# Head-column layout for the queries and keys kept in DRAM, and eight packing transfers in place of twelve

## The chip, the cores and the metric

The kernel runs on one core of a Trainium2 chip. The metric is the device time of one execution in microseconds. Before the change it is 2169.74 us, the median of three runs (2169.26 to 2172.96).

## The reference

Four layers in turn: attention, Fourier mixing, attention, Fourier mixing. Sequence S = 2048, width D = 640, 32 heads of 20 columns, float32. What is computed:

```python
def _A_ref(x, wqkv, wo):                       # sliding-window attention
    H = 32; Dh = D // H; W = 256
    qkv = (x @ wqkv).reshape(B, S, 3, H, Dh).transpose(2, 0, 3, 1, 4)
    q, k, v = qkv[0], qkv[1], qkv[2]
    scores = einsum("bhqd,bhkd->bhqk", q, k) * Dh ** -0.5
    mask = (idx[:, None] - idx[None, :] >= 0) & (idx[:, None] - idx[None, :] < W)
    p = softmax(where(mask, scores, -1e9))
    o = einsum("bhqk,bhkd->bhqd", p, v)
    return o.transpose(0, 2, 1, 3).reshape(B, S, D) @ wo

def _B_ref(x, cr, ci, hr, hi):                 # Fourier mixing
    a, b = einsum("bsd,ed->bse", x, hr), einsum("bsd,ed->bse", x, hi)
    return einsum("ts,bse->bte", cr, a) - einsum("ts,bse->bte", ci, b)

x = x + _A_ref(_layernorm(x), wqkv, wo)
x = x + _B_ref(_layernorm(x), cr, ci, hr, hi)
x = x + _A_ref(_layernorm(x), wqkv, wo)
x = x + _B_ref(_layernorm(x), cr, ci, hr, hi)
```

## The kernel before

Every operand of a product is held as two parts, an upper one (`hi`, rounded) and a lower one (`lo`, the remainder), and a product is three matmuls: hi by hi, hi by lo, lo by hi. All transfers are issued by one queue, SP's, in the order in which the program is written; an issue that waits holds everything behind it.

*Projection.* The query and key columns of the weight (1280 of them) are put in order ahead of the run by `arrange`: a quad is four heads and has 160 columns, 80 of queries and then 80 of keys, and within these the four heads' 20 columns one after the other. The product is made in ten chunks of 128 columns (`NCH`), each for four blocks of 512 sequence positions (`sb`), and lies transposed: a row is a weight column, and runs along the sequence. Chunks 0 and 1 are made by `piece` ahead of the heads, chunks 2 to 9 by `pieces` in between the heads' own matmuls (line 204). Each result is split into its two parts and stored in the DRAM tensor `qk` (named `qk_d` in the profile), which has the shape [2 parts, 1280 rows, 2048]. `store_qk` (line 504) stores both parts by one transfer of 512 KB; `pieces` (line 533) stores them by two of 256 KB, some half steps after the product (`post` counts half steps, `tick` runs what has come due).

*Packing.* The heads read a query tile `qp` and a key tile `kp`, two of each in turn over the quads. A tile has two halves of partitions, from 0 and from 64, for the two values of `e`; each half has three groups of 20 partitions: upper, lower, upper for queries, and upper, upper, lower for keys, so that one matmul over 60 rows gives all three products. Two heads (`z`) lie side by side in the columns. `pack(quad, sb)` makes the transfers for 512 positions of one quad: twelve, each of 20 partitions by two heads by 512 positions (line 563). Quad 0 is packed ahead of the heads, right after its pieces (`packed`). The others are packed eight steps ahead of their use (`due`, `AHEAD`), three transfers in each of four steps:

```python
for i, f in enumerate(self.pack(q, j)):
    defer(i // 3, f)
```

*Heads.* A step is one block of 128 positions of one quad, and there are 128 steps and ten more for the lead. In a step TensorE makes scores by query rows (`s_head`, line 606), of which VectorE takes masked row maxima (`mc`, line 611), and, ten steps later, scores by key rows (`t_head`, line 638), which ScalarE takes through the exponential (line 649), GpSimd masks (lines 655, 659) and TensorE multiplies with the values (`pv`, line 672). Once in four steps `m_rows` transposes the maxima of four blocks (line 618), ScalarE copies them with their sign changed (`mt`, line 622), and SP sends them by two small transfers (line 624, `qp<-mt`) into partitions 60 and 124 of the query tile; `kp` holds ones there, so the 61st row of the matmul in `t_head` takes the maximum off the score. The `t_head` matmul that needs them comes four steps later (six for the first of a quad).

In these four steps SP also issues: the row sums and the output of a block (`sm<-ou`, `o_d<-ou`, lines 695 and 696), the reciprocals (`r_d<-rc`, line 701), a load of values (`vq<-v_d`, line 590), the stores of line 533, loads of the next chunk's weight (line 480), and late in the phase loads for the output projection (lines 854, 860 and 945).

Each DMA has one of eight landing semaphores, taken in turn.

Of the kernel before, what the change touches and what calls it, by code (L numbers as in the profile page):

```python
# [7 lines left out]
F32 = mybir.dt.float32  # L8
# [9 lines left out]
P = 128  # L18
S = 2048
D = 640  # L20
KC = D // P
H = 32
DH = 20
NQ = H // 4
# [42 lines left out]
class Net:  # L67
    def __init__(self, nc, tc, ctx, a):
        self.nc, self.tc, self.a = nc, tc, a
        const = ctx.enter_context(tc.tile_pool(name="const", bufs=1))  # L70
        self.ln = ctx.enter_context(tc.tile_pool(name="ln", bufs=5))
        self.slots = ctx.enter_context(tc.tile_pool(name="slots", bufs=1))
        psum = ctx.enter_context(tc.tile_pool(name="psum", bufs=1, space=PSUM))
        self.work = ctx.enter_context(tc.tile_pool(name="work", bufs=2))
        dram = ctx.enter_context(tc.tile_pool(name="dram", bufs=1, space=DRAM))

        self.banks = psum.tile([P, 8, 512], F32, name="banks")

        def fixed(name, cols, dt):
            return const.tile([P, cols], dt, name=name)  # L80

        self.ident = fixed("ident", P, F32)
        self.mask = fixed("mask", 384, BF16)
        self.ones = const.tile([1, 128], F32, name="ones")
        nc.vector.memset(self.ones, 1.0)
        self.half = fixed("half", 1, F32)
        nc.vector.memset(self.half, -0.5)
        self.big, self.home = [None] * 4, [0, 1, 2, 3]
        self.qp, self.kp = [None] * 2, [None] * 2

        self.qk = dram.tile([2, 2 * D, S], F32, name="qk_d")
        self.vd = dram.tile([NQ, P, NB, 96], F32, name="v_d")
        self.ud = dram.tile([2, KC, P, S], F32, name="u_d")
        self.od = dram.tile([H, 32, S], F32, name="o_d")
        self.rd = dram.tile([NSB, H, 512], F32, name="r_d")
        self.td = dram.tile([2, KC, P, D], F32, name="t_d")
        self.xs = [dram.tile([S, D], F32, name=f"x_d{i}") for i in range(3)]
        self.turn = {}
        self.xn = {}
        self.ready, self.hid = 0, False  # L100
        self.slot = None
        self.posted = {}
        self.heavy = []
        self.left = 0
        self.tmp = None
# [389 lines left out]
    def piece(self, c, sb, role):  # L495
# [4 lines left out]
        self.split(st[:, 0, :], st[:, 1, :], p)  # L500
        self.store_qk(c, sb, st)

    def store_qk(self, c, sb, st):
        self.nc.sync.dma_start(
            self.qk[:, c * P:(c + 1) * P, sb * 512:(sb + 1) * 512].rearrange("l p s -> p l s"), st.bitcast(F32))

    def pieces(self, c, sbs, role):

        w = self.turn["w", c]
        sets, of = [], {}  # L510
        for sb in sbs:
            xt = self.xnt(sb)
            if sb % 2 == 0:
                sets.append(([], []))
            p = self.bank(role)
            of[id(p)] = p, sb, self.last_bank
            sets[-1][0].append(p)
            sets[-1][1].append([((w[:, 0, k, :], w[:, 1, k, :]), (xt[:, 0, k, :], xt[:, 1, k, :])) for k in range(KC)])

        lead = self.lead  # L520

        def copied(p, sb):
            d = 4 * (sb % 2) if not lead else 0
            hi = self.next_cc(512, 1536)
            r = self.raw()[:, :512]
            self.nc.scalar.activation(r, p, AF.Copy)
            self.post(1 + d, lambda: self.nc.gpsimd.tensor_copy(hi, r))
            self.post(2 if lead else 3 + d, lambda: self.nc.gpsimd.tensor_tensor(
                out=r.bitcast(F32R), in0=r, in1=hi.bitcast(F32), op=OP.subtract))

            def store():
                for l, x in enumerate((hi.bitcast(F32), r)):
                    self.nc.sync.dma_start(self.qk[l, c * P:(c + 1) * P, sb * 512:(sb + 1) * 512], x)
            self.post(3 if lead else 7 + d, store)
        for r in self.lockstep(sets):
            if isinstance(r, tuple):
                for p in r[1]:
                    p, sb, k = of[id(p)]
                    self.heavy.append((k, lambda p=p, sb=sb: copied(p, sb)))
                r = 0  # L540
            yield r
# [15 lines left out]
    def pack(self, quad, sb):  # L557

        todo = []
        cols = slice(sb * 512, (sb + 1) * 512)  # L560

        def put(d, src):
            self.nc.sync.dma_start(d.bitcast(F32), src)

        for kind in (1, 0):
            for e in range(2):
                r0 = 160 * quad + 80 * kind + 40 * e
                dst = (self.qp, self.kp)[kind][quad % 2].rearrange("p (z s) -> p z s", z=2)
                for part, l in enumerate(((0, 1, 0), (0, 0, 1))[kind]):
                    b = 64 * e + 20 * part  # L570
                    src = self.qk[l, r0:r0 + 40, cols].rearrange("(z r) s -> r z s", z=2)
                    todo.append(lambda d=dst[b:b + 20, :, cols], src=src: put(d, src))
        return todo

    def heads(self, xsrc, xdst, hook):
# [7 lines left out]
        def defer(d, fn):  # L583
            later.setdefault(now[0] + d, []).append(fn)
# [193 lines left out]
        todo = []  # L778
        for step in range(-LEAD, steps + 1):
            now[0] = step  # L780
            self.wide, self.lead, self.tiled = step + LEAD > steps, step < -2, step < steps - 1
            while todo:
                todo.pop(0)()
            for f in later.pop(step, []):
                f()
            s, t = step + LEAD, step
            if due and s >= due[0][0]:
                while done[0] < due[0][1]:
                    fill(15)
                due.pop(0)  # L790
                q, j = (s + AHEAD) // 16, (s + AHEAD) % 16 // 4
                for i, f in enumerate(self.pack(q, j)):
                    defer(i // 3, f)
                for f in later.pop(step, []):
                    f()
            if t > 0 and t % 4 == 0:
                load_v(t // 4 + 1)
            if done[0] < total:
                nf = max([FIRST if t < 0 else RATE]
                         + [(d - done[0]) / max(1, at - s) for at, d in due])  # L800
            elif made[0] < early:
                nf = LATE
            else:
                nf = LATE
            rows = ((s - 1) // 16, ((s - 1) % 16) // 4) if 4 <= s < steps + 4 and s % 4 == 0 else None
            for z in range(2):
                for e in range(2):
                    heads = [(t_head, t, e), (s_head, s, 1 - e)]
                    for head, n, i in heads[::-1] if e else heads:
                        if 0 <= n < steps:  # L810
                            head(n // 16, n % 16, z, i)
                    if 2 * t + z > 1 and t < FIVE and done[0] < total:
                        share()
                if z:
                    two = t <= FIVE
                    if t > 1 and not (two and t % 2):
                        v = t - 1 - two
                        todo.append(pv(v // 16, v % 16, 1 + two))
                        if self.heavy:
                            self.relieve()  # L820
                    if rows:
                        todo.append(m_rows(*rows))
                if 0 <= t < steps:
                    for e in range(2):
                        t_exp(t // 16, t % 16, z, e)
                    t_mask(t // 16, t % 16, z)
                if z:
                    relieve()
                    while todo and (not two or t < 2):
                        todo.pop(0)()  # L830
                if t < -1 or t >= steps or z == 0 and 0 <= t and (t >= FIVE or done[0] == total):
                    fill(nf)
                self.tick()
            if step > 16 * (NQ - 1):
                self.poll_late(step - 16 * (NQ - 1))
# [941 lines left out]
def arrange(A_x, A_wqkv, A_wo, B_dft_seq_re, B_dft_seq_im, B_dft_hid_re, B_dft_hid_im):  # L1777
# [5 lines left out]
    wqkv = np.asarray(A_wqkv)  # L1783
    cols = []
    for p in range(NQ):
        for kind in range(2):
            for e in range(2):
                for z in range(2):
                    b = kind * D + (4 * p + 2 * z + e) * DH
                    cols.extend(range(b, b + DH))  # L1790
    wqk = wqkv[:, cols].reshape(KC, P, NCH, P).transpose(2, 1, 0, 3)

    def rows(w):
# [40 lines left out]
```

## Time and profile before

| what | value |
|---|---|
| median of three runs | 2169.74 us |
| the profiled execution's own time | 2169.5 us |
| its span, first to last instruction | 2167.7 us |
| mean granted TensorE clock | 0.992 |
| TensorE busy | 2108.8 us, 97% |
| VectorE, ScalarE, GpSimd busy | 1596.9, 1153.9, 925.3 us |
| moved by DMA | 395.21 MB, mean 182 GB/s |

The two attention layers lie at about 0 to 520 us and 1058 to 1600 us; the heads, with the packing beside them, at about 155 to 520 and 1236 to 1600. SP issues transfers and is not among the busy engines; its own times are in the timeline of its queue, where a row gives start, duration and the number of issues merged. The duration of an issue includes what it is held for. A row of waits gives the waiting line, what ended the wait, the total in us, the number of waits and the longest.

### The profile page before, as it was taken

Reading aid. Unit: us, or ns where it says so; the run is one execution under the profiler, and the core shown is the slowest. Engines: PE = TensorE matmul, PEld = TensorE weight load, DVE = VectorE, ACT = ScalarE, POOL = GpSimd, SP = SyncE. Lnnn points to the kernel's source line nnn. Section 1 sums busy time; section 2 is a strip of 40 time slices with the busy share of each in tenths; the row PEclk is TensorE's granted clock in tenths of the full one; section 3 lists DMA queues with packets and bytes.
Section 4 is the critical chain, followed back from the end, with each engine's and each line's share of the span. In section 5 each row is a group of like instructions: output and inputs, shape, how many; then the busy total and the mean of one; then the engine's idle time right before and its main releaser. Section 6 shows DMA issues by size and latency. Waiting matters only on the chain.

```text
span 2167.7 us, 46148 instructions
## 1 busy us (share of the span) xinstructions
PE 2108.8 (97%) x16405; PEld 1749.2 (81%) x16405; DVE 1596.9 (74%) x3936; ACT 1153.9 (53%) x2511; POOL 925.3 (43%) x1455
## 2 busy tenths in 40 slices
PE   8999999999999999999999999999999999999999
PEld 8987776677878888889999877766777788888899
DVE  7358777676897968777751578876778869687777
ACT  3228877666554545543431288776665545455522
POOL 2047776766423234130230487777654323241300
PEclk9999999999999999999999999999999999999999
DMA  6556666786445454757645466667864464546653
GB/s 210 169 162 184 202 191 207 206 229 199 140 125 178 134 180 127 230 193 259 213 143 185 152 186 202 200 205 225 230 183 134 126 189 136 165 149 218 221 177 125
DMA packets 222630, 395.21 MB, mean 182 GB/s; under 512 B 40384, under 2 KB 86976, under 8 KB 222400
## 3 DMA queue, kind: packets, MB, share of 16 engines
q1 hardware_dynamic: 222400, 392.26, 58.3%
q8 instruction: 130, 2.13, 0.4%
q14 instruction: 100, 0.82, 0.1%
HBM read 273.94 MB, written 117.05 MB: 180 GB/s over the span
## 4 chain that ended last, share of the span: by engine, by line
PE 78%; DVE 7%; DMA 5%; ACT 4%; POOL 4%; issue 2%; SPq 1%; ACTq 0%; DVEq 0%; POOLq 0%
PE banks L1373 27%; PE banks L186 15%; PE banks L204 12%; PE banks L672 7%; PE banks L1628 6%; PE banks L638 5%; PE banks L606 4%; DMA qp<-mt 3%; POOL big L179 1%; POOL ou L1303 1%; DVE qp L179 1%; PE banks L286 1%; ACT big L1023 1%; DMA pt<-c 1%; POOL rs L1073 1%
## 5 line engine op out<-in xcount | busy, mean ns | idle before, releaser
L611 DVE CUSTOM_DVE_ANT_0 banks<-banks,mask 128x384 f32<-128x384 f32 (+2 forms) x1024 | 515.0, 566 | 175.5 <-PE banks L606 140.1
L649 ACT ACTIVATE pt<-banks 128x384 f32<-128x384 f32 (+2 forms) x864 | 363.0, 472 | 100.9 <-PE banks L638 47.8
L638 PE MATMUL banks<-qp,kp 61*128 61x384 f32 (+2 forms) x1024 | 336.6, 366 | 19.4 <-DMA qp<-mt 18.2
L606 PE MATMUL banks<-kp,qp 60*128 60x384 f32 (+2 forms) x1024 | 337.4, 370 | 5.4 <-DVE mc L611 4.5
L204 PE MATMUL banks<-big,wc 64*128 64x512 f32 x1920 | 338.4, 398 | 0.4 <-DVE pt L419 0.4
L655 POOL TENSOR_SCALAR_AFFINE_SELECT pt<-pt 128x256 f32<-128x256 f32 x432 | 177.4, 412 | 148.6 <-ACT pt L649 123.8
L638 PEld LDWEIGHTS banks<-qp,kp 61*128 61x128 f32 x1024 | 178.7, 187 | 63.6 <-issue 25.2
L606 PEld LDWEIGHTS banks<-kp,qp 60*128 60x128 f32 x1024 | 174.1, 187 | 58.1 <-DVE mc L611 41.9
L204 PEld LDWEIGHTS banks<-big,wc 64*128 64x128 f32 x1920 | 199.1, 188 | 12.3 <-DVE pt L419 0.5
L1303 POOL TENSOR_TENSOR pt<-pt,pt 128x512 f32<-128x512 f32 x36 | 62.9, 1747 | 289.3 <-DMA pt<-c 176.1
L672 PE MATMUL banks<-pt,vq 128*32 128x128 f32 (+1 forms) x3664 | 178.4, 317 | 1.3 <-POOL pt L655 1.2
L173 ACT ACTIVATE cc<-pt 128x512 fp32r<-128x512 f32 x150 | 94.0, 626 | 155.0 <-POOL pt L1279 52.7
L173 ACT ACTIVATE qp<-pt 128x512 fp32r<-128x512 f32 (+1 forms) x195 | 119.6, 624 | 94.2 <-DVE pt L1304 46.4
L179 DVE TENSOR_TENSOR cc<-pt,cc 128x512 fp32r<-128x512 f32 x150 | 120.1, 811 | 53.5 <-ACT cc L173 51.1
L659 POOL TENSOR_SCALAR_AFFINE_SELECT pt<-pt 128x256 f32<-128x256 f32 x380 | 156.6, 412 | 0.0
L1373 PE MATMUL banks<-qp,big 128*128 128x512 f32 x630 | 151.1, 391 | 5.0 <-DVE qp L179 4.0
L179 DVE TENSOR_TENSOR qp<-pt,qp 128x512 fp32r<-128x512 f32 (+1 forms) x195 | 147.6, 770 | 10.4 <-ACT qp L173 7.7
L672 PEld LDWEIGHTS banks<-pt,vq 128*32 128x32 f32 x3664 | 101.3, 111 | 61.0 <-issue 22.7
L611 DVE DVE_READ_ACCUMULATOR2_ANT mc<- 128x1 f32 x1024 | 146.3, 143 | 0.0
L1373 PEld LDWEIGHTS banks<-qp,big 128*128 128x128 f32 x630 | 117.0, 188 | 31.0 <-DVE qp L179 5.7
L1373 PE MATMUL banks<-qp,xc 128*128 128x512 f32 x480 | 118.0, 391 | 2.0 <-DVE xc L179 1.5
L1373 PEld LDWEIGHTS banks<-qp,xc 128*128 128x128 f32 x480 | 89.8, 188 | 22.6 <-DVE xc L179 2.4
(232 smaller groups left out, 4561.5 us busy)
## 6 DMA issues: line engine op xcount, KB each, us to landing
pt<-c SPq DMA_DIRECT2D x188, 512.0 KB
kp<-qk_d SPq DMA_DIRECT2D x384, 80.0 KB
qp<-qk_d SPq DMA_DIRECT2D x384, 80.0 KB
kp<-u_d SPq DMA_DIRECT2D x32, 640.0 KB
qk_d<-cc SPq DMA_DIRECT2D x64, 256.0 KB
qk_d<-x SPq DMA_DIRECT2D x64, 256.0 KB
o_d<-ou SPq DMA_DIRECT2D x64, 256.0 KB
x_d<-x SPq DMA_DIRECT2D x48, 320.0 KB
```

Of the source, the lines that this page charges most:

```text
L173: nc.scalar.activation(hi, src, AF.Copy, scale=-1.0 if neg else 1.0)
L179: (eng or nc.vector).tensor_tensor(out=lo, in0=src, in1=hi.bitcast(F32), op=OP.subtract)
L186: self.nc.tensor.matmul(p, x, y, start=n == 0, stop=n == last)
L204: self.nc.tensor.matmul(ps[a], x[r], y[r], start=half + i == 0, stop=half == 1 and i == n - 1, skip_group_check=True)
L606: nc.tensor.matmul(p, qp[quad % 2][b:b + 60, z, qb * P:(qb + 1) * P], kp[quad % 2][b:b + 60, z, k0 * P:(qb + 1) * P], start=True, stop=True)
L611: nc.vector.tensor_tensor_reduce(out=p, in0=p, in1=self.mask[:, 384 - n * P:], scale=1.0, scalar=NEG, op0=OP.add, op1=OP.max, accum_out=mc ...
L638: nc.tensor.matmul(self.banks[:, tb[e], :n * P], kp[quad % 2][b:b + 61, z, kb * P:(kb + 1) * P], qp[quad % 2][b:b + 61, z, kb * P:(kb + n) ...
L649: nc.scalar.activation(pt[quad, kb][:, 2 * z + e, :n * P], self.banks[:, tb[e], :n * P], AF.Exp, scale=SCALE)
L655: nc.gpsimd.affine_select(out=t[:, :, 0:P], in_=t[:, :, 0:P], pattern=[[0, 2], [1, P]], compare_op=OP.is_ge, fill=0.0, base=0, channel_mul ...
L659: nc.gpsimd.affine_select(out=t[:, :, 256:384], in_=t[:, :, 256:384], pattern=[[0, 2], [-1, P]], compare_op=OP.is_gt, fill=0.0, base=0, ch ...
L672: nc.tensor.matmul(p[32 * h:32 * h + 32, (c0 - qa) * P:(c1 - qa) * P], vq[:, 96 * (kb % 4) + 21 * h:96 * (kb % 4) + 21 * h + 32], t[:, h, ...
L1373: nc.tensor.matmul(self.banks[:, bk, :], p, b[q], start=start and m == 0, stop=stop and last and m == 2, skip_group_check=True)
```

## The change

The DRAM tensor for queries and keys becomes [8 quads, 2 parts, 160 rows, 2048 + 512]: a quad's two parts lie behind each other, and a row is longer than what is used of it. The weight's columns are ordered by head column first: row d x 8 + g of a quad is column d of the head g, where g counts kind (query, key), `e` and `z`. A head's upper and its lower rows are then one sequence of 40 rows, eight apart, so that one transfer of 40 partitions fills two neighbouring groups of a tile; the third group is filled by one of 20 partitions. A pack has eight transfers, two in each of the four steps. A chunk of 128 rows that lies over two quads is now stored by a transfer (or a pair) for each.

```diff
-        self.qk = dram.tile([2, 2 * D, S], F32, name="qk_d")
+        self.qk = dram.tile([NQ, 2, 8 * DH, S + 512], F32, name="qk_d")
...
+    def rows_of(self, c):
+        n, r0, r1 = 8 * DH, c * P, (c + 1) * P
+        for q in range(r0 // n, -(-r1 // n)):
+            a, b = max(r0, q * n), min(r1, q * n + n)
+            yield q, a - q * n, a - r0, b - r0
+
     def store_qk(self, c, sb, st):
-        self.nc.sync.dma_start(
-            self.qk[:, c * P:(c + 1) * P, sb * 512:(sb + 1) * 512].rearrange("l p s -> p l s"), st.bitcast(F32))
+        for q, r0, a, b in self.rows_of(c):
+            self.nc.sync.dma_start(
+                self.qk[q, :, r0:r0 + b - a, sb * 512:(sb + 1) * 512].rearrange("l p s -> p l s"),
+                st[a:b].bitcast(F32))
...
             def store():
-                for l, x in enumerate((hi.bitcast(F32), r)):
-                    self.nc.sync.dma_start(self.qk[l, c * P:(c + 1) * P, sb * 512:(sb + 1) * 512], x)
+                for q, r0, a, b in self.rows_of(c):
+                    for l, x in enumerate((hi.bitcast(F32), r)):
+                        self.nc.sync.dma_start(self.qk[q, l, r0:r0 + b - a, sb * 512:(sb + 1) * 512], x[a:b])
...
+        src = self.qk[quad].rearrange("l (r g) s -> (l r) g s", g=8)
         for kind in (1, 0):
             for e in range(2):
-                r0 = 160 * quad + 80 * kind + 40 * e
                 dst = (self.qp, self.kp)[kind][quad % 2].rearrange("p (z s) -> p z s", z=2)
-                for part, l in enumerate(((0, 1, 0), (0, 0, 1))[kind]):
-                    b = 64 * e + 20 * part
-                    src = self.qk[l, r0:r0 + 40, cols].rearrange("(z r) s -> r z s", z=2)
-                    todo.append(lambda d=dst[b:b + 20, :, cols], src=src: put(d, src))
+                g = 4 * kind + 2 * e
+                for part, n in (((0, 2), (2, 1)), ((0, 1), (1, 2)))[kind]:
+                    b = 64 * e + DH * part
+                    todo.append(lambda d=dst[b:b + DH * n, :, cols], src=src[:DH * n, g:g + 2, cols]: put(d, src))
...
-                    defer(i // 3, f)
+                    defer(i // 2, f)
...
     for p in range(NQ):
-        for kind in range(2):
-            for e in range(2):
-                for z in range(2):
-                    b = kind * D + (4 * p + 2 * z + e) * DH
-                    cols.extend(range(b, b + DH))
+        for d in range(DH):
+            for kind in range(2):
+                for e in range(2):
+                    for z in range(2):
+                        cols.append(kind * D + (4 * p + 2 * z + e) * DH + d)
```

## The prediction

> **What bounds the kernel now.** The page comes first: the span, and the chain that ended last.
>
> ```profile
> span 2167.7 us, 46148 instructions
> ...
> PE 78%; DVE 7%; DMA 5%; ACT 4%; POOL 4%; issue 2%; SPq 1%; ACTq 0%; DVEq 0%; POOLq 0%
> ```
>
> TensorE carries the chain, so an edit that touches no matmul can gain only where TensorE stands still. Next the stretches of the two attention layers in which heads are computed and packing runs (columns: PE, PEld, DVE, ACT, POOL busy, granted clock, DMA share, GB/s).
>
> ```profile
> 155.00:250.00 95.00, 94.85 (x1115) 69.68 (x1117) 78.11 (x310) 77.16 (x192) 72.34 (x163) 0.98 0.66 200
> 250.00:350.00 100.00, 94.87 (x1145) 69.21 (x1147) 76.50 (x308) 76.30 (x192) 75.13 (x166) 1.00 0.66 192
> 350.00:450.00 100.00, 92.15 (x1070) 65.08 (x1063) 68.30 (x267) 66.87 (x168) 74.78 (x147) 0.93 0.72 213
> 1236.00:1330.00 94.00, 93.77 (x1099) 68.55 (x1102) 77.66 (x309) 75.48 (x188) 71.44 (x161) 0.98 0.66 199
> 1330.00:1440.00 110.00, 106.94 (x1298) 77.98 (x1294) 86.10 (x345) 87.06 (x217) 84.04 (x186) 1.00 0.65 196
> 1440.00:1535.00 95.00, 86.53 (x1032) 61.70 (x1024) 64.33 (x249) 62.00 (x155) 69.70 (x136) 0.93 0.76 220
> ```
>
> TensorE is hardly idle in the first stretch of each layer and loses 24.9 us in the six stretches together, nearly all in the later four. The waits of TensorE name the cause:
>
> ```profile
> PE banks L638 <- DMA qp<-mt: 18.2, 14, 2.6
> ...
> PE banks L606 <- DVE mc L611: 4.5, 10, 1.0
> ```
>
> `qp<-mt` is the pair of 4 KB transfers that put the negated row maxima into the query tile; the score matmul of line 638 cannot start without them. Three timelines (ScalarE, SP's queue, TensorE) show why they are late: ScalarE makes `mt` once in four steps, and SP issues the pair.
>
> ```profile
> 173.34 0.25 ACT L622 ACTIVATE mt<-banks 16x128 fp32r<-16x128 f32 x1
> ...
> 265.35 0.25 ACT L622 ACTIVATE mt<-banks 16x128 fp32r<-16x128 f32 x1
> ...
> 286.08 0.25 ACT L622 ACTIVATE mt<-banks 16x128 fp32r<-16x128 f32 x1
> ```
>
> ```profile
> 173.62 1.11 SPq L624 DMA_DIRECT2D qp<-mt  x2
> ...
> 268.67 2.21 SPq L624 DMA_DIRECT2D qp<-mt  x2
> ...
> 281.07 2.94 SPq L563 DMA_DIRECT2D kp<-qk_d  x3
> 284.13 0.35 SPq L701 DMA_DIRECT2D r_d<-rc  x1
> 284.58 0.37 SPq L533 DMA_DIRECT2D qk_d<-cc  x1
> 285.05 0.38 SPq L533 DMA_DIRECT2D qk_d<-x  x1
> 285.47 1.40 SPq L563 DMA_DIRECT2D qp<-qk_d  x3
> 286.97 0.34 SPq L590 DMA_DIRECT2D vq<-v_d  x1
> 287.36 1.13 SPq L563 DMA_DIRECT2D qp<-qk_d  x3
> 288.58 0.34 SPq L533 DMA_DIRECT2D qk_d<-cc  x1
> 289.03 0.38 SPq L533 DMA_DIRECT2D qk_d<-x  x1
> 289.49 0.62 SPq L695 DMA_DIRECT2D sm<-ou  x1
> 290.16 0.78 SPq L696 DMA_DIRECT2D o_d<-ou  x1
> 291.01 1.42 SPq L563 DMA_DIRECT2D kp<-qk_d  x3
> 292.53 1.08 SPq L624 DMA_DIRECT2D qp<-mt  x2
> ```
>
> ```profile
> 294.61 0.41 PE L638 MATMUL banks<-qp,kp 61*128 61x384 f32 x1 [1.54 <-DMA qp<-mt]
> ```
>
> SP issues without a pause between 281.07 and 292.53: it is a queue with a backlog. At 173 us the pair leaves 0.03 us after `mt` is ready (173.34 + 0.25), at 268.67 it is 3.07 late, at 292.53 it is 6.19 late, and TensorE stands 1.54 us. From the first to the last of these rows lie eleven periods of four steps: TensorE's side (ScalarE's rows) takes 112.74 / 11 = 10.25 us a period, SP's 118.91 / 11 = 10.81. SP falls behind by 0.56 us a period until TensorE has to wait for it. How late SP may be follows from the stall: without it the matmul would have started at 294.61 - 1.54 = 293.07; the pair took 2.08 from issue to use, so an issue by 290.99, 4.65 us after `mt`, costs nothing.
>
> **The change, part by part.** The rows of the issues it touches, with min/median/max ns:
>
> ```profile
> L563 SPq DMA_DIRECT2D kp<-qk_d x384: 273/342/1327, 43.1 to 1538.2; - x192
> L563 SPq DMA_DIRECT2D qp<-qk_d x384: 273/336/1552, 47.1 to 1545.4; - x192
> L533 SPq DMA_DIRECT2D qk_d<-cc x64: 319/347/1488, 131.2 to 1511.6; - x64
> L533 SPq DMA_DIRECT2D qk_d<-x x64: 319/376/1078, 132.6 to 1512.1; - x64
> L504 SPq DMA_DIRECT2D qk_d<-cc x16: 359/365/393, 36.6 to 1183.7; - x16
> ```
>
> Packing: 768 transfers (64 packs of twelve) become 512. The bytes stay, 960 KB a pack, and so does the 2 KB piece; four of the eight are now 160 KB. Whether a doubled transfer costs more to issue: 80 KB takes 0.34, 256 KB 0.35 to 0.38 and 512 KB 0.37, so 0.34 stands. With the gap of 0.05 inside a group ((1.13 - 3 x 0.34) / 2) a removed issue is worth 0.39; four a period make 1.56 us. The four groups stay in the same four steps (keys of the even heads, keys of the odd, then queries); the `mt` pair stands behind the first group, so one issue fewer is ahead of it there and three elsewhere.
>
> Stores: a chunk has 128 rows and a quad 160, so of ten chunks those numbered 1, 2, 3, 6, 7 and 8 lie over two quads and are stored in two pieces. On line 533 that is five of eight chunks, 40 of 64 pairs, 80 issues more; on line 504 eight more. Each costs 0.36 and the 0.1 to the next row: 0.46. They come in bunches: while chunks 6 to 8 are projected (about 265 to 385 us and 1345 to 1475 us) there are four more in two periods, elsewhere in the heads none after chunk 3.
>
> So SP needs per period, outside those two stretches, 10.81 - 1.56 = 9.25 against 10.25: its backlog shrinks by 1 us a period, and the wait goes. Inside them it is 10.81 - 1.56 + 2 x 0.46 = 10.17: next to no drift. The stalls lie so (waits of TensorE within 265 to 385 and within 1345 to 1475):
>
> ```profile
> PE banks L638 <- DMA qp<-mt: 6.9, 5, 2.6
> ```
>
> ```profile
> PE banks L638 <- DMA qp<-mt: 6.6, 5, 1.7
> ```
>
> 13.5 of 18.2 us lie in the stretches with split stores, 4.7 outside. The 4.7 I count as gained whole. For the 13.5 the bounds are nothing and all. Lateness at their entry was 3.07 and rose by 3.12 to 6.19; with a drained backlog it enters at about 1 and the same swing ends near 4.1, under the 4.65 allowed. That is close, so I take seven tenths: 9.5.
>
> Some long stalls are followed by a stretch of half clock (the first is shown with the stretch before it, then the last; a third lies at 1474.3):
>
> ```profile
> 368.40:371.80 3.40, 0.82 (x7) 0.38 (x4) 0.96 (x4) 0.52 (x2) 1.28 (x4) 1.00 0.30 89
> 371.80:375.20 3.40, 3.40 (x26) 2.40 (x28) 2.39 (x9) 1.96 (x4) 0.99 (x3) 0.50 0.83 257
> ...
> 1528.90:1532.30 3.40, 3.40 (x39) 2.27 (x37) 1.31 (x7) 1.34 (x4) 1.28 (x4) 0.50 0.66 208
> ```
>
> 3.4 us at 0.50 lose at most 1.7: three make 5.1 at most. The last lies outside the split stretches (1.7), the other two by seven tenths give 2.4: 4.1. The Trainium skill, "TensorE: Matmul & The Clock Gate", Part 1, has the clock halved after an idle window of about 3.4 us. Here the window before was busy for 0.82 us, so by the letter of the page stalls are not the cause and the 4.1 stay lost: the time would be 4.1 us higher.
>
> What takes the place of the waits: DVE's maxima (4.5 us in ten waits, above) and the exponentials behind them, in step with TensorE once it no longer pauses; I give back 2.0 (between 0 and the 4.5).
>
> Before the heads each pack of quad 0 follows its stores at once. Its first key transfers needed chunk 0 alone and now need chunk 1 too, so SP waits one group earlier for the same landing, with eight transfers behind it instead of nine. Behind SP in line are only loads and value stores; TensorE is covered by the products of line 186 (below), and the first score matmul comes after them. Cost nothing; without that cover the wait is at most a store's issue and landing, which the pair at 292.53 puts near 2 us, eight times: 16 us.
>
> ```profile
> 80.11 37.83 PE banks L186 x225
> ```
>
> Later packs read chunks whose stores were issued periods before; the order of the weight's columns is settled ahead of the run. Both cost nothing.
>
> Sum: 4.7 + 9.5 + 4.1 - 2.0 = 16.3 less. The profiled execution took 2169.5 us (1.8 outside its span), 0.24 under the median 2169.74: 2153.2, so 2153.
>
> **Rivals.** *The split stores eat it.* SP's backlog inside the two stretches stays as it is, and only the 4.7 and its 1.7 of clock go: 2163. For it speaks the drift of 0.08 us, which is no margin; against it the lower entry.
>
> *Nothing moves.* The group at 281.07 took 2.94 instead of 1.13: SP is also held until earlier transfers land. If that holding, not issuing, sets its pace, a transfer of twice the rows lands later, and fewer issues wait longer each: 2169.5. It decides if each of the remaining issues is held 0.1 us longer (1.56 over some sixteen a period). Against it, most groups of three in the rows take 1.1 to 1.4. The Trainium skill, "DMA: Bandwidth & Descriptors", "Issuing engines are not separate DMA queues", speaks for this rival: it calls the sequencer's time to start a transfer usually small beside the transfer. The trace disagrees so far as SP's rows are back to back.
>
> *Slower: the new layout slows the reads.* Rows lie 10 KB apart instead of 8 KB, and one transfer steps 80 KB from partition to partition. At 200 GB/s a period moves 2.05 MB, packing 0.98 of it, so 0.32 of the DMA share of 0.66. The engines are full when packing's part doubles (0.34 + 0.65). At 2.3 times a period becomes 10.25 x 1.08 = 11.0: 0.8 us over some 58 periods, 46 us: 2216. Against it: each piece is still 2 KB long. The same page, "Why a DMA increments its semaphore by 16 and not by 1", would put 20 rows and 40 rows alike on ten of the sixteen engines; by an estimate from that, a rise by three tenths would do.
>
> **How the numbers follow.** Stalls mostly gone: 0.64, 2145 to 2160 by itself (all 18.2 + 5.1 would be 2146.2). Split stores eat it: 0.15. Nothing moves: 0.12. Slower: 0.09. A measurement of this kernel can tell about 0.2%, 4.3 us. The first two are faster, which gives 0.79, the third same, 0.12, the last slower, 0.09. The range goes from 2144 (all, with a little for the time that restarting costs) to 2166 (the second with half its gain) and leaves out the last two.
>
> **What would show it.** SP: groups of two in place of three, 0.34 each; four stores in a row between 265 and 385. The wait of line 638 for `qp<-mt` falls from 18.2 to 4 or so, in the two stretches only; the pair at about 290 us leaves under 4.6 us after `mt`. TensorE loses under 10 us in the six stretches. Half clock after 371 and 1529 is gone if stalls cause it. I am wrong if packing groups are held over 0.5 us an issue, if the DMA share of the stretches rises above 0.7, or if the waits of line 638 stay at 18.

## The result, and the profile after

The changed kernel takes 2145.03 us (median of four runs, 2144.12 to 2146.5) against 2171.35 for the kernel before in the same series: a ratio of 0.988 (95% interval 0.9863 to 0.9897), 26 us less. Forecast were 2153 us, 17 less, with a range of 2144 to 2166, so the time lies 1 us above the lower end of the range. The profiled execution took 2145.41 us with a span of 2143.5 us, 24.2 less than the span before.

The page of the changed kernel, first lines and chain:

```profile
span 2143.5 us, 45993 instructions
...
PE 2097.7 (98%) x16405; PEld 1744.3 (81%) x16405; DVE 1590.2 (74%) x3936; ACT 1153.4 (54%) x2511; POOL 931.7 (43%) x1455
...
PE 81%; DVE 7%; POOL 4%; ACT 3%; DMA 2%; issue 1%; SPq 0%; DVEq 0%; ACTq 0%; POOLq 0%
```

DMA's share of the chain falls from 5% to 2%. TensorE is idle for 2143.5 - 2097.7 = 45.8 us, where it was 58.9 before. Its waits, in the order of the answer (lines from 533 on have moved by nine: 638 is now 647, 606 is 615, 563 is 572):

```profile
PE banks L647 <- DMA qp<-mt: 5.8, 4, 2.5
...
PE banks L615 <- DVE mc L620: 3.8, 8, 1.0
```

The waits for `qp<-mt` fall from 18.2 us in fourteen to 5.8 in four. The heads of the second attention layer begin some 16 us sooner than before, so its stretches below are moved by that much.

```profile
155.00:250.00 95.00, 94.77 (x1126) 69.56 (x1124) 78.79 (x316) 77.94 (x193) 73.31 (x165) 1.00 0.68 209
250.00:350.00 100.00, 100.00 (x1232) 73.56 (x1231) 80.58 (x327) 81.64 (x206) 79.22 (x177) 1.00 0.71 203
350.00:450.00 100.00, 96.19 (x1192) 70.11 (x1190) 74.39 (x287) 69.67 (x175) 78.19 (x152) 0.95 0.82 232
1220.00:1314.00 94.00, 93.78 (x1116) 68.75 (x1116) 77.82 (x312) 76.96 (x191) 72.66 (x163) 1.00 0.69 213
1314.00:1424.00 110.00, 108.23 (x1319) 79.48 (x1316) 87.63 (x354) 87.30 (x220) 85.08 (x189) 1.00 0.69 199
1424.00:1519.00 95.00, 89.58 (x1141) 64.96 (x1137) 69.47 (x269) 65.73 (x164) 73.72 (x143) 0.96 0.80 228
```

From 250 to 350 us TensorE does not stand still at all; before it lost 5.1 us there. In the six stretches together it loses 11.5 us instead of 24.9. The four waits that are left, first those within 262 to 380 us and then those within 1329 to 1459 us:

```profile
PE banks L647 <- DMA qp<-mt: 1.5, 1, 1.5
```

```profile
PE banks L647 <- DMA qp<-mt: 4.3, 3, 2.5
```

All lie where split stores fall. ScalarE's and SP's timelines around the place that stood for the kernel before:

```profile
283.27 0.25 ACT L631 ACTIVATE mt<-banks 16x128 fp32r<-16x128 f32 x1
```

```profile
273.91 1.09 SPq L633 DMA_DIRECT2D qp<-mt  x2
275.05 0.81 SPq L572 DMA_DIRECT2D kp<-qk_d  x2
275.96 0.35 SPq L710 DMA_DIRECT2D r_d<-rc  x1
276.41 0.36 SPq L542 DMA_DIRECT2D qk_d<-cc  x1
276.86 0.37 SPq L542 DMA_DIRECT2D qk_d<-x  x1
277.29 0.42 SPq L542 DMA_DIRECT2D qk_d<-cc  x1
277.75 0.43 SPq L542 DMA_DIRECT2D qk_d<-x  x1
278.23 2.33 SPq L572 DMA_DIRECT2D qp<-qk_d  x2
280.66 0.34 SPq L599 DMA_DIRECT2D vq<-v_d  x1
281.05 0.75 SPq L572 DMA_DIRECT2D qp<-qk_d  x2
281.89 0.32 SPq L542 DMA_DIRECT2D qk_d<-cc  x1
282.31 0.37 SPq L542 DMA_DIRECT2D qk_d<-x  x1
282.73 0.41 SPq L542 DMA_DIRECT2D qk_d<-cc  x1
283.19 0.44 SPq L542 DMA_DIRECT2D qk_d<-x  x1
283.73 0.61 SPq L704 DMA_DIRECT2D sm<-ou  x1
284.38 0.48 SPq L705 DMA_DIRECT2D o_d<-ou  x1
284.90 1.12 SPq L572 DMA_DIRECT2D kp<-qk_d  x2
286.12 1.11 SPq L633 DMA_DIRECT2D qp<-mt  x2
```

The groups of two and the stores in fours are there. The pair leaves 286.12 - 283.52 = 2.6 us after `mt`; before, its counterpart was 6.19 late. This is a period with two split stores: SP needs 12.2 us for it, more than TensorE's 10.25, and makes it good in the next (the next pair leaves at 293.71, 7.6 later). The group at 278.23 shows the other cost: 2.33 us for two issues, so SP was held.

### The profile page after: what moved, and what is told of

The parts are those of the page before. It is cut to its first block, busy times and chain, and to the rows that moved or that the text cites. A ratio compares the mean times of both kernels' runs of the same rounds, so it can differ in the third digit from the quotient of the medians.

```text
span 2143.5 us, 45993 instructions
## 1 busy us (share of the span) xinstructions
PE 2097.7 (98%) x16405; PEld 1744.3 (81%) x16405; DVE 1590.2 (74%) x3936; ACT 1153.4 (54%) x2511; POOL 931.7 (43%) x1455
## 2 busy tenths in 40 slices
DMA packets 221477, 395.19 MB, mean 184 GB/s; under 512 B 39232, under 2 KB 85824, under 8 KB 221248
## 4 chain that ended last, share of the span: by engine, by line
PE 81%; DVE 7%; POOL 4%; ACT 3%; DMA 2%; issue 1%; SPq 0%; DVEq 0%; ACTq 0%; POOLq 0%
PE banks L1382 28%; PE banks L186 15%; PE banks L204 14%; PE banks L681 7%; PE banks L1637 6%; PE banks L615 5%; PE banks L647 5%; POOL big L179 1%; POOL ou L1312 1%; DVE qp L179 1%; PE banks L286 1%; ACT big L1032 1%; DVE banks L620 1%; POOL rs L1082 1%; PE banks L627 1%
## 5 line engine op out<-in xcount | busy, mean ns | idle before, releaser
L620 DVE CUSTOM_DVE_ANT_0 banks<-banks,mask 128x384 f32<-128x384 f32 (+2 forms) x1024 | 513.6, 564 | 156.8 <-PE banks L615 124.0
L179 DVE TENSOR_TENSOR qp<-pt,qp 128x512 fp32r<-128x512 f32 (+1 forms) x195 | 149.0, 777 | 10.7 <-ACT qp L173 8.2
```

The costliest lines, as they stand in the source:

```text
L179: (eng or nc.vector).tensor_tensor(out=lo, in0=src, in1=hi.bitcast(F32), op=OP.subtract)
L620: nc.vector.tensor_tensor_reduce(out=p, in0=p, in1=self.mask[:, 384 - n * P:], scale=1.0, scalar=NEG, op0=OP.add, op1=OP.max, accum_out=mc ...
```

## The experiments

Three theories of why the change helps were put against each other. *Queue*: SP has a backlog, and fewer issues remove it. *Layout*: the new rows make the transfers quicker. *Landing*: SP is held by transfers under way, so bytes count and not the number. A fourth, *place*, has the pair late only because of the three transfers just ahead of it.

**The layout alone, with twelve transfers.**

```diff
-                for part, n in (((0, 2), (2, 1)), ((0, 1), (1, 2)))[kind]:
+                for part, l in enumerate(((0, 1, 0), (0, 0, 1))[kind]):
...
-  todo.append(lambda d=dst[b:b + DH * n, :, cols], src=src[:DH * n, g:g + 2, cols]: put(d, src))
+  todo.append(lambda d=dst[b:b + DH, :, cols], src=src[DH * l:DH * l + DH, g:g + 2, cols]: put(d, src))
...
-                    defer(i // 2, f)
+                    defer(i // 3, f)
```

> The changed kernel with its layout and its split stores, but each pack again as twelve transfers of 20 partitions, three in each of four steps. Queue theory (SP's queue has a backlog and every issue costs it 0.4 us): SP needs per period what it needed before, 10.81 us, and 0.92 more in the stretches with split stores, 1.5 over TensorE's 10.25 there; the waits for qp<-mt rise from 18 to 35 us or more, about 2185 us (2176 to 2198). Layout theory (longer rows or the new order of rows make the transfers quicker): the gain stays, about 2145 us.

Measured: 2186.11 us, ratio to before 1.0085 (1.0061 to 1.0109). Its waits of TensorE:

```profile
PE banks L647 <- DMA qp<-mt: 25.9, 13, 3.1
```

The layout with its split stores costs 17 us; what the layout does without them is seen two experiments on. The waits rose less than I had put (25.9, not 35), but the granted clock fell too, to 0.986 from 0.992. Merging the transfers is worth some 41 us from there.

**The longer row.**

```diff
-        self.qk = dram.tile([NQ, 2, 8 * DH, S + 512], F32, name="qk_d")
+        self.qk = dram.tile([NQ, 2, 8 * DH, S], F32, name="qk_d")
```

> The changed kernel with rows of 2048 in place of 2048 + 512, so that rows lie 8 KB apart and a transfer's partitions 64 KB. Queue theory: the same count of issues, so the same time, 2145 us (2142 to 2149). Layout theory: the longer row is what helps, and without it the time goes back by 8 us or more, 2153 or higher, with a higher DMA share in the heads.

Measured: 2147.29 us (2142.51 to 2149.2), ratio 0.9899 (0.9877 to 0.9921); its waits for `qp<-mt` are 6.1 us. The interval holds the changed kernel's 0.988, so no effect of the distance of rows shows here. This run leaves the change from 8 KB to 64 KB between a transfer's partitions as it is.

**The split stores alone, on the kernel before.**

```diff
-                for l, x in enumerate((hi.bitcast(F32), r)):
-                    self.nc.sync.dma_start(self.qk[l, c * P:(c + 1) * P, sb * 512:(sb + 1) * 512], x)
+                for r0, r1, a, b in self.rows_of(c):
+                    for l, x in enumerate((hi.bitcast(F32), r)):
+                        self.nc.sync.dma_start(self.qk[l, r0:r1, sb * 512:(sb + 1) * 512], x[a:b])
```

(and `store_qk` likewise)

> The kernel before, with its layout and its twelve transfers, but with the stores of chunks 1, 2, 3, 6, 7 and 8 cut in two at the quads' borders, as the change cuts them. Queue theory: two issues more a period in the stretches of chunks 6 to 8, 0.92 us each period on a queue that is already 0.56 short; waits for qp<-mt 30 to 40 us, 2180 to 2195 us. Landing theory: as many bytes in smaller transfers that land sooner, no change, 2169 to 2174 us.

Measured: 2195.69 us, ratio 1.0125 (1.0105 to 1.0144).

```profile
PE banks L646 <- DMA qp<-mt: 32.0, 15, 4.9
```

88 issues more, not a byte more, 27 us more. This is the price of the split stores, and landing theory's "no change" is out.

This kernel and the one with twelve transfers have the same number of issues of every kind and differ in the layout alone, and they were timed in one series: 2195.69 us here (2193.81 to 2196.75), 2186.11 with the new layout (2183.18 to 2192.1). The runs of the two do not overlap, so the layout theory has a part: the new order of rows is worth some 10 us beside split stores. It does not slow the reads, as the prediction's slower rival had it. SP's waits for landings (the rows of its queue's waits that a transfer ended, from 155 to 500 and from 1220 to 1590 us) sum to 57 us here and 44 there; whether that is how the layout helps is not shown. The change is then the sum of three: 27 us lost by the split stores, some 10 gained by the layout, some 41 gained by the merging, 24 us in all by that series.

**Issues without bytes, on the changed kernel.**

```diff
+        self.spare = const.tile([DH, 4, 2, 16], F32, name="spare")
...
                     defer(i // 2, f)
+                for i in range(4):
+                    src = self.qk[q].rearrange("l (r g) s -> (l r) g s", g=8)[:DH, 2 * i:2 * i + 2, j * 512:j * 512 + 16]
+                    defer(i, lambda i=i, src=src: nc.sync.dma_start(self.spare[:, i], src))
```

> The changed kernel with four further transfers a pack, one in each of the four steps, of 20 partitions by two pieces of 64 bytes into a tile that nothing reads: the count of issues of before comes back, next to no bytes do. Queue theory: as with twelve real transfers, SP falls behind again, 2170 to 2195 us, waits for qp<-mt over 15 us. Landing theory (SP is held by the bytes of transfers that have not landed, not by their number): the added ones land at once and cost little, 2145 to 2152 us.

Measured: 2198.13 us, ratio to before 1.0128 (1.0098 to 1.0158).

```profile
PE banks L648 <- DMA qp<-mt: 31.5, 17, 4.5
```

Only the packs of quads 1 to 7 pass through this loop, so these are 224 tiny transfers (7 quads, four packs, four transfers, two layers):

```profile
L806 SPq DMA_DIRECT2D spare<-qk_d x224: 273/338/1768, 150.3 to 1573.5; - x112
```

With the split stores SP issues 56 transfers more than before the change. The tiny ones cost 53 us over the changed kernel and bring the waits back. Each takes the queue as long to issue as one of 80 KB (0.34 us), which is 76 us in all. The number of issues counts.

**The same issues, fewer bytes, on the kernel before.**

```diff
-                    todo.append(lambda d=dst[b:b + 20, :, cols], src=src: put(d, src))
+                    n = 128 if part == 2 and quad > 1 else 512
+                    todo.append(lambda d=dst[b:b + 20, :, sb * 512:sb * 512 + n], src=src[:, :, :n]: put(d, src))
```

> The kernel before with twelve transfers a pack, but from quad 2 on the third transfer of each group brings 128 of its 512 positions (the rest of that group of partitions is left as it was): the same number of issues, a quarter less of the packing's bytes. Queue theory: the time stays near before, 2163 to 2172 us. Landing theory: SP is held for a shorter time by transfers under way, and the waits for qp<-mt fall by half or more, 2150 to 2160 us.

Measured: 2152.82 us (2148.05 to 2153.58), ratio 0.9911 (0.9883 to 0.994).

```profile
PE banks L639 <- DMA qp<-mt: 3.2, 4, 1.4
```

Here the queue theory in its bare form falls: with as many issues as before, fewer bytes take away most of the waits and 16 us. The traces show two ways. SP is held less: a wait for a landing stands in its queue as a pause before an issue, and its waits that a transfer ended (same stretches as above) sum to 64 us before and 40 here, about 0.35 us a period. So the 10.81 us that SP needed for a period held two parts, the issues and the time for which it waits for landings. And the pair itself lands sooner. It leaves as late after `mt` as before (3.9 us in the median in both, up to the end of its second issue); but at the four waits that are left it took 1.8 to 2.6 us from issue to use, at the fourteen of before 2.1 to 5.7. What each of the two is worth is not separated.

**The same cut on the changed kernel.**

```diff
+                    w = 128 if n == 1 and quad > 1 else 512
-  todo.append(lambda d=dst[b:b + DH * n, :, cols], src=src[:DH * n, g:g + 2, cols]: put(d, src))
+  todo.append(lambda d=dst[b:b + DH * n, :, sb * 512:sb * 512 + w], src=src[:DH * n, g:g + 2, sb * 512:sb * 512 + w]: put(d, src))
```

> The changed kernel, but from quad 2 on each transfer of 20 partitions brings 128 of its 512 positions (the rest is left as it was): eight issues as in the changed kernel, a quarter less of the packing's bytes. If SP is still held by landings in the changed kernel, the waits for qp<-mt fall from 5.8 to under 2 us: 2137 to 2143 us. If with eight transfers only the number of issues in the split stretches is left, the time stays at 2143 to 2147.

Measured: 2139.03 us (2137.23 to 2145.52), ratio to before 0.9866 (0.9847 to 0.9885). No wait for `qp<-mt` is among TensorE's waits any more, and in two of its stretches TensorE does not pause:

```profile
250.00:350.00 100.00, 100.00 (x1234) 73.59 (x1232) 80.55 (x328) 81.66 (x205) 79.27 (x177) 1.00 0.63 180
350.00:450.00 100.00, 95.91 (x1245) 70.59 (x1241) 76.80 (x296) 72.04 (x184) 81.24 (x157) 1.00 0.75 224
1236.00:1330.00 94.00, 94.00 (x1157) 68.69 (x1157) 76.58 (x307) 76.75 (x193) 73.48 (x165) 1.00 0.63 190
```

SP's waits for landings sum to 38 us here and to 69 in the changed kernel. The time is 6 us lower, but the two intervals overlap (four of the five runs lie under every run of the changed kernel), so it is likely, and not shown, that landings still cost the changed kernel something. The waits agree with it: 5.8 us there, none here.

**The pair's place in the line, on the kernel before.**

```diff
-                    defer(i // 3, f)
+                    defer(1 + i // 3, f)
```

> The kernel before, with each group of packing transfers one step later, so that the pair qp<-mt stands ahead of the first group instead of behind it; the issues are the same. Queue theory: SP's rate sets the pace once it has fallen behind, so the order changes only how far it may fall behind; most of the waits remain, 2162 to 2171 us. Place theory (the pair is late because of the three transfers just ahead of it): it leaves 1.2 us earlier, most of the 14 waits are no longer than that, 2148 to 2157 us.

Measured: 2175.5 us (2170.64 to 2179.17), ratio 1.0026 (1.0011 to 1.0041). The profile is of the quickest of its ten runs.

```profile
PE banks L638 <- DMA qp<-mt: 12.0, 9, 2.6
...
PE banks L606 <- DMA kp<-qk_d: 3.3, 5, 2.0
```

The pair is late less often, and in exchange the packs come late, for which the other score matmul (line 606) waits. Two causes are mixed here: this version issues the packs a step later by itself, and a queue that is short as a whole passes its lateness on to whoever stands last. Either way the place in the line does not cure it. That it came out a little slower than before I had not expected.

**The same on the changed kernel.**

```diff
-                    defer(i // 2, f)
+                    defer(1 + i // 2, f)
```

> The changed kernel with each group of packing transfers one step later, so that the pair qp<-mt stands ahead of the first group. Queue theory: where SP has room, the place in the line counts; the four waits that are left (5.8 us in all, all in the stretches with split stores) lose 0.8 us each or more, and one or two half-clock windows may go with them: 2138 to 2144 us. If the remaining waits are made by the four stores in a row and not by the group, the time stays at 2145.

Measured: 2145.8 us (2143.28 to 2146.22), ratio 0.9881 (0.9854 to 0.9908): no different from the changed kernel.

```profile
PE banks L615 <- DMA qp<-qk_d: 1.2, 3, 0.6
...
PE banks L647 <- DMA qp<-mt: 1.4, 2, 0.8
```

The waits for the pair did fall, by 4.4 us, and 1.2 came back for the packs; but none of it is in the time. In the profiled executions TensorE's idle time fell from 45.8 to 42.8 us, and its busy time rose from 2097.7 to 2101.1. The granted clock was 0.994 where the changed kernel's was 0.995, which may be about 2 us of that. My expectation failed here, and the rest of that difference is open.

**The pair issued by ScalarE, on the changed kernel.**

```diff
-                    nc.sync.dma_start(qp[quad % 2][60:125:64, z, u * 512:(u + 1) * 512].bitcast(F32),
+                    nc.scalar.dma_start(qp[quad % 2][60:125:64, z, u * 512:(u + 1) * 512].bitcast(F32),
```

> The changed kernel with the pair qp<-mt issued by ScalarE right after it has made mt, so that it no longer stands in SP's line. Queue theory: SP has two issues of 0.55 us fewer a period, and the four waits that are left go; but ScalarE pays about 1 us a period for the issues and is held when the landing semaphore that the pair takes in turn still belongs to a transfer under way, which delays the exponentials behind it. If it is held for less than 1 us, 2138 to 2145 us; if for 2 us or more, 2150 us or above with TensorE waiting for ScalarE.

Measured: 2234.93 us, ratio to before 1.029 (1.0256 to 1.0324).

```profile
PE banks L647 <- ACT pt L658: 33.4, 47, 2.9
```

TensorE now waits for the exponentials. I had put such a time down to a ScalarE that is held for 2 us or more, and that is not what the trace shows: in 57 of the 64 periods ScalarE has issued both transfers within 1.4 us of `mt`, and in five it is held for more than 1 us. What it pays in every period is the issuing itself, 1.1 us ahead of the exponentials. The one that is held is SP, since the landing semaphores go round in the order of the program and it must wait for the pair's:

```profile
SPq L572 <- DMA qp<-mt: 86.7, 44, 4.3
```

In the changed kernel that row is 0.3 us, one wait. So ScalarE was mostly in the case for which I had put 2138 to 2145 us, and the time is 90 us above the changed kernel's; the 90 us are not divided here between ScalarE's issuing and SP's waits.

**One transfer of 60 rows.**

```diff
-        self.qk = dram.tile([NQ, 2, 8 * DH, S + 512], F32, name="qk_d")
+        self.qk = dram.tile([NQ, 4, 8 * DH, S + 512], F32, name="qk_d")
...
                         self.nc.sync.dma_start(self.qk[q, l, r0:r0 + b - a, sb * 512:(sb + 1) * 512], x[a:b])
+                    self.nc.sync.dma_start(
+                        self.qk[q, 2:4, r0:r0 + b - a, sb * 512:(sb + 1) * 512].rearrange("l p s -> p l s"),
+                        hi[a:b].bitcast(F32).unsqueeze(1).broadcast_to([b - a, 2, 512]))
...
-                for part, n in (((0, 2), (2, 1)), ((0, 1), (1, 2)))[kind]:
-  ...
+                todo.append(lambda d=dst[64 * e:64 * e + 60, :, cols],
+                            src=src[DH * (1 - kind):DH * (1 - kind) + 60, g:g + 2, cols]: put(d, src))
...
-                    defer(i // 2, f)
+                    defer(i, f)
```

> The changed kernel with four stored parts (upper, lower, upper, upper) in place of two, so that one transfer of 60 rows fills all three groups of a half: the keys take the parts 0 to 2, the queries 1 to 3. Four transfers a pack in place of eight, one in each step; for it each piece is stored by three transfers in place of two, the third with twice the bytes. Queue with holds (SP's time is issues plus what it is held by transfers that have not landed): in the stretches with split stores four issues fewer in two periods, elsewhere three fewer a period; what is left of the waits for qp<-mt (5.8 us) goes, with one to three half-clock windows: 2134 to 2143 us. If the doubled bytes of the stores hold SP for as long as the saved issues free it, 2145 or more.

Measured: 2186.49 us, ratio to before 1.0083 (1.0065 to 1.0101).

```profile
PE banks L652 <- DMA qp<-mt: 34.0, 9, 6.6
```

Two of its stretches:

```profile
155.00:250.00 95.00, 86.84 (x1003) 62.82 (x1004) 69.49 (x277) 68.55 (x171) 68.95 (x149) 0.96 0.85 251
250.00:350.00 100.00, 93.69 (x1117) 68.89 (x1115) 76.78 (x309) 76.44 (x191) 72.48 (x163) 0.98 0.88 245
```

Fewer issues than any other version and yet slow. The third part's stores bring 42 MB more (437.13 in place of 395.19), the DMA share rises from 0.68 and 0.71 to 0.85 and 0.88, and SP's issues take longer: line 542's stores took 416 and 419 ns in the median, the same stores here 453 and 502. SP is then late. At eight of the nine waits the pair left 5 to 9 us after `mt`; at the longest, eight stores and four packing transfers stand between `mt` and the pair (ScalarE's row, then SP's):

```profile
163.68 0.25 ACT L636 ACTIVATE mt<-banks 16x128 fp32r<-16x128 f32 x1
```

```profile
172.87 1.06 SPq L638 DMA_DIRECT2D qp<-mt  x2
```

The case that I had put for 2145 us or more came true, and by more than I thought. Whether the bytes or the bunching of the stores does more of it is not separated.

None of these versions that computes the whole is faster than the changed kernel beyond its interval.

## Why the prediction was right, point by point

| term | forecast, us | measured, us |
|---|---|---|
| waits for `qp<-mt` outside the split stretches | 4.7 | 4.7 (none left) |
| waits inside them | 9.5 of 13.5 | 7.7 (5.8 left) |
| half clock | 4.1 | 6.6 |
| given back to other waits | -2.0 | +0.7 |
| not foreseen | 0 | 4.5 |
| sum, on the span | 16.3 | 24.2 |

*What bounds it.* Right. TensorE waited for the pair, and the pair for SP's queue. Taking issues away removes the waits, adding issues (with the split stores, with twelve transfers, with tiny ones) brings them back, in five kernels. Issues are not all: fewer bytes take the waits away too, and the version of 60 rows, with fewer issues and more bytes, has more of them.

*The stalls.* Right in place and nearly in size: outside the stretches with split stores nothing is left, and all four that remain are inside, as the balance of 10.17 against 10.25 had it (the period above with split stores and the next take 9.9 each on average). But the allowance was wrong. I took from one stall that an issue up to 4.65 us after `mt` costs nothing, with 2.08 from issue to use; of the fourteen waits before, that one has the shortest. The longest, 2.58 us at 371.40, belongs to a pair that left only 3.64 after `mt` and took over 5 us to land (ScalarE's row, then the chain's):

```profile
361.86 0.25 ACT L622 ACTIVATE mt<-banks 16x128 fp32r<-16x128 f32 x1
```

```profile
365.75 5.51 DMA qp<-mt
```

Eight of the fourteen pairs left within 4.65 us. So a late issue and a slow landing add up, and the seven tenths that I took for the split stretches (9.5; measured 7.7) rested on the first alone. That it came near is in part luck.

*The price of an issue.* Right in effect, wrong in what it is made of. I wrote 10.81 as if it were issues at 0.4 us. The kernel with fewer bytes shows that holding was part of it, so the second rival named a mechanism that is real. It lost because in the changed kernel SP was held for about as long in sum (69 us of waits for landings, 64 before): groups like that at 278.23 (2.33 for two) stand beside many of 0.75, as those at 281.07 (2.94 for three) stood beside 1.1 before. The issue of a doubled transfer takes what I put, and that of a short store a little more:

```profile
L572 SPq DMA_DIRECT2D kp<-qk_d x256: 273/350/1362, 44.0 to 1511.9; - x128
L572 SPq DMA_DIRECT2D qp<-qk_d x256: 273/351/1924, 46.1 to 1518.6; - x128
L542 SPq DMA_DIRECT2D qk_d<-cc x104: 318/416/1314, 131.5 to 1487.0; - x104
L542 SPq DMA_DIRECT2D qk_d<-x x104: 304/419/2005, 132.9 to 1487.4; - x104
```

*The clock.* Near in size, and by luck. I counted three stretches of half clock, 5.1 us. The granted clocks in my own table of six stretches already come to about 17 us, ten such stretches. By the mean granted clock, 0.992 of 2167.7 us before and 0.995 of 2143.5 after, 17.3 us were lost and 10.7 are (six such stretches): 6.6 fewer. Of the three that I counted, each after a wait for the pair, only one has gone (1.7 us): after the change two waits are still followed by one, at 374.2 and at 1442.6 (the stretch before it, and then it):

```profile
1439.00:1442.50 3.50, 1.55 (x14) 1.24 (x14) 0.90 (x7) 1.05 (x3) 2.59 (x5) 1.00 0.57 175
1442.60:1446.00 3.40, 3.40 (x37) 1.92 (x38) 0.39 (x4) 1.28 (x5) 1.99 (x5) 0.50 0.96 217
```

The Trainium skill, "TensorE: Matmul & The Clock Gate", Part 1, would ask for an idle window; here the window was busy for 1.55 us. The rest of the 6.6 comes from stretches that follow no wait for the pair, at 156.8 and 1238.8 for instance, and what sets those off is open. The kernels go the same way, 0.998 with no wait for the pair and 0.985 to 0.988 with 26 to 34 us of them. But these waits are not the only cause: the kernel before with fewer bytes has 3.2 us of them and still 0.993, and the four runs of the changed kernel differ from 0.994 to 0.998 while their times differ by 2.4 us. A lost clock is therefore not a loss of time one for one, and the 6.6 in the table is a count and not a measured price.

*Given back.* This step failed in sign. I took 2.0 us for the other waits of the heads. TensorE's idle time fell by 13.1, 0.7 more than the waits for the pair. DVE's part fell from 4.5 to 3.8 instead of rising. That these waits came after stalls and went with them would explain it, and is not shown.

*Not foreseen.* TensorE's busy time fell by 11.1 us, of which the clock explains 6.6. The matmuls of the heads are shorter on average (line 638 took 366 ns and takes 363, line 204 took 398 and takes 395), but that is the clock again: outside the stretches of half clock line 638 takes 361 and 362, line 204 takes 395 in both. Where the other 4.5 lie is not settled; with a mean clock rounded to three digits, each of the two losses above is known to about 1 us.

*A sign that came up.* I wrote that I would be wrong if the DMA share of the stretches rose above 0.7. It is 0.71, 0.82 and 0.80 in three of them, and two had been at 0.72 and 0.76 before. The sign was badly set: when TensorE stands less, the same bytes move in less time (213 GB/s before and 232 after in the third stretch), and the share rises with success. It rose by more than the rate did, though, and why is open.

## What to carry to other kernels

A queue that issues every transfer is a resource like an engine: add up its rows for one period of the schedule and compare with the bound engine's, because a shortfall of 5% shows only as another transfer that is late now and then. When such a queue is short, moving the urgent item forward did not help here; taking out issues, or bytes that it waits for, did. A change that saves issues in one place and adds them in another is to be counted stretch by stretch, and the next limit (here, as it seems, the bytes, at a DMA share near 0.85) belongs in the count before more bytes are traded for fewer issues.

## What the runs showed of the hardware that was not expected

224 transfers of 2.5 KB each, next to nothing in bytes, cost 53 us on this queue, which is more than the whole change had gained. And a quarter fewer of the packing's bytes from quad 2 on, with an unchanged number of issues, gained 16 us: near its limit the queue reacts to both. A transfer of 40 partitions took the queue no longer to issue than one of 20 (medians of 337 to 356 ns against 344 to 375 in the changed kernel). Issuing the pair from ScalarE did not free SP: the two queues share the landing semaphores, and SP waited 86.7 us in line 572 for the pair.
